# Two products of the receptances in one VectorE instruction, masks by comparison, and a new order of the work, in a linear-attention kernel followed by a token mixer

## The chip, the cores and the metric

The kernel runs on one core of a Trainium2 chip. The time is the device time of one execution in microseconds (us). The kernel before has a median of 104.82 us in three runs (104.32 to 105.43). The profile is of one execution, which took 104.46 us. Its span, from the first to the last recorded work, is 102.6 us, so that 1.86 us of that execution lie around the span.

Engine names in the profile: PE is TensorE (PEld its weight loads), DVE is VectorE, ACT is ScalarE, POOL is GpSimd, SP is SyncE, which here issues nearly all of the transfers (DMA). PSUM is the memory that TensorE writes to; SBUF is the main memory on the core.

## What is computed

```python
# r, k, v, w: (4, 8, 768, 48) f32;  u: (8, 48)
state = zeros((B, H, D, D))
for t in range(S):
    cur = einsum('bhd,bhe->bhde', u[None] * kt, vt)
    y[:, :, t] = einsum('bhd,bhde->bhe', rt, state + cur)
    state = wt[:, :, :, None] * state + einsum('bhd,bhe->bhde', kt, vt)
x = y.transpose(0, 2, 1, 3).reshape(B, S, H * D)
W_tok = einsum('bsd,btd->bst', x @ w_q, x @ w_k) / sqrt(64)
out = maximum(einsum('bst,btd->bsd', W_tok, x), 0) @ w_out
```

The sequential state is replaced by chunks of 128 tokens: inside a chunk the products of r and k are a masked matrix, between chunks a state is carried.

## The kernel before, in words

The four batches have 768 tokens each. A unit is 256 tokens (two chunks, called c = 0 and 1) of one batch, with all eight heads, so that there are twelve units, 0 to 11, three for each batch. `unit` (L493) adds the steps of one unit to a plan; after the third unit of a batch it also adds the mixer of that batch (T, TS, mx, rl, fp, os, st). The first and the last unit are cut in two halves ("split") for most steps. The last four units (`PAIRS`, L236) load k and r with another assignment of tokens to partitions, and need a second set of masks and scales (CM2, US2, gx2, gv2, gk2).

The steps of a unit that matter here, with the buffer that each one writes:

- Loads of w, k, r, v into wg, kg, rg, vg: all on SP's queue, L306, L312 and L320. Each has a ring of four buffers. In units 0 to 7, k and r come in two halves; in units 8 to 11, v comes in four quarters.
- ln (L525): lw <- log of w, on ScalarE. cw (L549): running sums of lw by a product with the mask CM (or CM2). ep and en (L569, L575): the exponentials of plus and minus those sums, on ScalarE. ew (L582): a small copy inside ep, on GpSimd, not in units 8 to 11.
- k16 and r16 (L539, L536): casts of k and r to bf16. kT and rT (L591): their transposes on TensorE, left in PSUM.
- ks (L610, run in the helper at L437 or L443): copy of kT from PSUM to SBUF. qT = rT * ks (L614, VectorE). RT = rT * ep (L624, VectorE). KT = ks * en (L633, GpSimd or VectorE).
- v16, vp, VB (L649, L657, L661): v cast, put in order by a product with the permutation PM, and copied from PSUM; in units 8 to 11 only one cast (L644). dps, dd (L667, L674): sums of qT with u. Vd = VB * dd (L681, GpSimd).
- A (L693): products of KT and RT. AM (L701, VectorE): A times the mask US (or US2). kb, kd (L708, L714): KT transposed back and copied with the scale gk into a padded buffer. sn, SB (L732, L748): the carried state. yi, ya: products into the output of the unit. X (L807, VectorE): that output with Vd added, then xt, XT, qk, QK for the mixer.

Every name above is a ring of a few buffers (`RINGS`, L260), mostly two: a step that fills a buffer waits until the readers of the buffer two units back are done.

The order on each engine is not that of the program text. `Plan.add` (L47) records a step with the engines that may run it and an estimated duration; `Plan.order` (L80) plays all the queues, takes on each engine the steps in order of a written number (`RANK`, L165), and gives out PSUM banks. Where a step may run on several engines, the next letter of `ALT` (L202) chooses (A ScalarE, D VectorE, P GpSimd). L453 to L457 tell the plan at which time each engine comes out of set-up. `WARM` products of zeros (L944, "z") fill gaps on TensorE, beside nine in set-up.

`setup` (L325) makes the constants. VectorE sets Z, CM, IDP and ID to start values, makes the positions, clears the pads of lw, k, r, and clears PM and the pads of the two kd buffers (L368 to L371: the long one is 16 pieces of 80 bf16). GpSimd makes iotas and cuts CM, IDP and ID by affine selects (L344, L349, L357). Four further functions are steps of the plan and run on GpSimd where `RANK` puts them: the positions of the second set (L381), its masks (L392), its scales (L405, VectorE) and the permutation PM (L373).

Of the kernel before, what the change touches and what calls it, by code (L numbers as in the profile page):

```python
# [10 lines left out]
F32 = mybir.dt.float32  # L11
# [22 lines left out]
class Plan:  # L34
# [131 lines left out]
    0, 0, 0, 0, 63, 33, 0, 0, 33, 1, 2, 3, 14, 2, 5, 22, 13, 0, 0, 0, 1, 0, 0, 2, 0, 0, 3, 0, 0,  # L166
    4, 0, 0, 8, 0, 0, 1, 1, 2, 1, 3, 4, 4, 5, 7, 6, 4, 6, 3, 5, 6, 4, 7, 6, 9, 17, 11, 28, 16, 15,
    18, 12, 8, 16, 10, 10, 8, 21, 14, 23, 12, 25, 15, 26, 37, 34, 33, 21, 57, 33, 82, 46, 5, 0, 0,
    6, 0, 0, 7, 0, 0, 9, 0, 0, 10, 0, 0, 12, 0, 0, 7, 8, 11, 11, 9, 10, 10, 15, 20, 9, 13, 11, 12,
    13, 32, 19, 38, 22, 22, 27, 16, 31, 18, 29, 18, 36, 20, 40, 22, 43, 46, 53, 49, 29, 66, 35,  # L170
    84, 43, 11, 0, 0, 13, 0, 0, 14, 0, 0, 15, 0, 0, 16, 0, 0, 20, 0, 0, 12, 14, 16, 24, 17, 17,
    15, 30, 35, 17, 19, 23, 19, 20, 45, 25, 50, 28, 26, 54, 30, 48, 27, 42, 24, 52, 28, 61, 63,
    64, 65, 37, 76, 42, 88, 45, 91, 48, 100, 51, 105, 54, 78, 0, 0, 106, 55, 138, 70, 67, 0, 0,
    118, 60, 160, 81, 81, 0, 0, 18, 0, 0, 17, 0, 0, 19, 0, 0, 24, 0, 0, 25, 0, 0, 26, 0, 0, 20,
    21, 24, 39, 24, 23, 23, 41, 56, 25, 32, 31, 26, 25, 58, 31, 62, 35, 32, 71, 40, 68, 38, 51,
    29, 59, 33, 69, 39, 73, 77, 81, 75, 44, 104, 53, 120, 63, 23, 0, 0, 21, 0, 0, 22, 0, 0, 27, 0,
    0, 29, 0, 0, 30, 0, 0, 26, 21, 27, 55, 30, 28, 32, 47, 60, 27, 34, 36, 31, 29, 67, 36, 79, 43,
    37, 78, 42, 83, 47, 74, 41, 80, 45, 87, 48, 90, 93, 96, 95, 52, 113, 62, 125, 64, 32, 0, 0,
    28, 0, 0, 31, 0, 0, 37, 0, 0, 38, 0, 0, 40, 0, 0, 34, 30, 41, 72, 38, 35, 39, 70, 86, 37, 50,
    49, 36, 38, 97, 50, 99, 54, 46, 101, 55, 92, 51, 94, 49, 102, 57, 111, 115, 112, 114, 63, 122,  # L180
    67, 139, 71, 145, 75, 154, 78, 172, 86, 82, 0, 0, 157, 80, 191, 98, 83, 0, 0, 171, 85, 201,
    101, 80, 0, 0, 35, 0, 0, 34, 0, 0, 36, 0, 0, 39, 0, 0, 44, 0, 0, 42, 0, 0, 40, 34, 39, 89, 47,
    42, 46, 85, 98, 44, 53, 58, 43, 45, 116, 58, 117, 59, 52, 109, 60, 124, 68, 107, 59, 121, 66,
    127, 69, 131, 136, 133, 135, 72, 144, 78, 153, 77, 47, 0, 0, 41, 0, 0, 43, 0, 0, 45, 0, 0, 46,
    0, 0, 50, 0, 0, 52, 40, 41, 108, 56, 47, 57, 103, 119, 56, 65, 64, 49, 48, 123, 62, 126, 65,
    53, 142, 77, 132, 71, 128, 66, 134, 73, 140, 76, 149, 151, 155, 152, 82, 168, 84, 186, 93, 51,
    0, 0, 48, 0, 0, 53, 0, 0, 54, 0, 0, 57, 0, 0, 68, 0, 0, 58, 0, 0, 61, 44, 51, 130, 67, 68,
    110, 137, 61, 74, 75, 54, 60, 146, 79, 62, 150, 81, 147, 80, 143, 73, 161, 86, 164, 166, 167,
    169, 90, 173, 88, 182, 91, 193, 99, 200, 100, 218, 110, 84, 0, 0, 212, 105, 226, 114, 85, 0,
    0, 215, 107, 229, 115, 86, 0, 0, 52, 0, 0, 49, 0, 0, 59, 0, 0, 55, 0, 0, 65, 0, 0, 69, 0, 0,  # L190
    70, 0, 0, 69, 50, 57, 141, 74, 72, 129, 156, 70, 84, 83, 56, 61, 175, 87, 65, 165, 89, 176,
    94, 159, 85, 163, 88, 174, 93, 177, 179, 181, 183, 97, 203, 102, 211, 104, 64, 0, 0, 56, 0, 0,
    61, 0, 0, 60, 0, 0, 76, 0, 0, 62, 0, 0, 71, 0, 0, 79, 55, 59, 162, 83, 82, 148, 170, 76, 91,
    92, 63, 64, 185, 92, 67, 188, 98, 180, 95, 178, 89, 184, 96, 189, 99, 192, 198, 194, 197, 105,
    204, 103, 214, 106, 75, 0, 0, 66, 0, 0, 79, 0, 0, 72, 0, 0, 74, 0, 0, 77, 0, 0, 73, 0, 0, 90,
    58, 66, 187, 95, 94, 96, 97, 158, 190, 87, 101, 100, 68, 102, 69, 70, 196, 104, 71, 72, 199,
    106, 206, 108, 195, 103, 202, 107, 205, 208, 207, 209, 210, 213, 109, 216, 111, 219, 222, 109,
    111, 110, 217, 112, 220, 221, 108, 112, 223, 225, 224, 113, 227, 113, 114, 231, 232, 117, 118,
    87, 0, 0, 89, 0, 0, 228, 115, 116, 233, 236, 118, 120, 88, 0, 0, 91, 0, 0, 230, 117, 116, 234,
    235, 119, 119, 121, 90, 0, 0, 2, 3, 5, 7, 8, 9, 13, 14, 18, 19, 44,  # L200
]
ALT = "ADDDDPAAAAADPPDPAAAAAPPDPAADAAAAAAAAAAPDDADAAAPPAPADDDAPAAPADADAAAAAAAAPPAPAADDAPPDPAAAAAPPDPDAAAAAAADAAPPDPADAAPPAPAAAAPPDPPDDDAADAADAAADDDAADADA"  # L202

WARM = 11
# [3 lines left out]
def kernel(  # L208
# [27 lines left out]
    PAIRS = (8,9,10,11)  # L236
# [56 lines left out]
    gx = const([C, 1], F32, "gx")  # L293
    gv = const([C, 1], F32, "gv")
    gk = const([C, 1], F32, "gk")

    US2 = const([C, C], F32, "US2")
    CM2 = const([C, 2 * C], BF16, "CM2")
    pos2 = const([C, 1], I32, "pos2")
    pos3 = const([C, 1], I32, "pos3")  # L300
    gx2 = const([C, 1], F32, "gx2")
    gv2 = const([C, 1], F32, "gv2")
    gk2 = const([C, 1], F32, "gk2")

    def load(b, i, tl, ap):
# [680 lines left out]
```

## Time and profile before

| what | before |
|---|---|
| median of three runs | 104.82 us |
| the profiled execution | 104.46 us |
| its span | 102.6 us |
| busy PE / DVE / ACT / POOL | 90.2 / 83.3 / 80.1 / 77.4 us |
| share of all DMA engines' time, the loads' queue | 83.0% |
| AM on DVE | 24 of 1220 ns |
| KT on POOL | 9 of 2127 ns, 3 halves of 1158 ns |
| KT on DVE | 1 of 1923 ns, 1 half of 426 ns |
| qT and RT on DVE, 1024 columns | 12 of 683 ns and 10 of 684 ns |

A line of a timeline has the start and the duration in us, the engine, the line of the kernel, the operation and what it writes and reads; a bracket at its end is the idle time before it and what ended that. A line of the chain has the start, the time and the place, and the chain is that of the work that ended last, followed back from the end. In the slices of the span, each digit is the busy share of a fortieth of the span, in tenths.

### The profile page before, as it was taken

The numbers are of one execution on the slowest core, as the hardware profiler recorded it, in microseconds if no ns is written. First come the engines' busy times: TensorE is split into PE (matmuls) and PEld (weight loads), VectorE is DVE, ScalarE is ACT, GpSimd is POOL, SyncE is SP. The second block draws the span as 40 slices with busy tenths as digits, with TensorE's granted clock in tenths as the row PEclk, the third lists the DMA queues.
The fourth block names the chain that finished last, engine by engine and source line by source line (L and its number), as shares of the span: only waits on it lengthen the run. The fifth ranks groups of instructions, "written<-read, shape, count | busy, mean of one in ns | idle before, by whom it ended". The sixth has DMA issues, their size and how long they took to land.

```text
span 102.6 us, 4039 instructions
## 1 busy us (share of the span) xinstructions
PE 90.2 (88%) x1647; PEld 67.8 (66%) x1648; DVE 83.3 (81%) x144; ACT 80.1 (78%) x124; POOL 77.4 (75%) x100
## 2 busy tenths in 40 slices
PE   5978698997969999999999999978999999999910
PEld 1245467765947878777789886756888677967600
DVE  6768799999999999799998989885989977738410
ACT  6375789999789969999898989756998949774730
POOL 5899999999999999999898997469886992000000
PEclk9999999999999999999999999999999999999996
DMA  2999999999999999799999999967970001954892
GB/s 39 287 294 347 334 333 276 323 336 327 322 289 299 336 318 301 217 290 320 250 238 215 209 225 233 311 121 136 292 224 11 0 0 50 364 209 160 310 369 90
DMA packets 46595, 24.65 MB, mean 240 GB/s; under 512 B 39152, under 2 KB 46448, under 8 KB 46576
## 3 DMA queue, kind: packets, MB, share of 16 engines
q1 hardware_dynamic: 46416, 24.19, 83.0%
q8 instruction: 13, 0.21, 0.7%
q10 hardware_dynamic: 160, 0.20, 0.5%
q14 instruction: 6, 0.05, 0.2%
HBM read 19.66 MB, written 4.72 MB: 238 GB/s over the span
## 4 chain that ended last, share of the span: by engine, by line
PE 49%; DVE 14%; DMA 8%; POOL 8%; ACT 6%; issue 6%; SPq 4%; POOLq 0%; ACTq 0%; DVEq 0%
PE PS L243 49%; DMA rg<-in_r_dram 5%; DVE AM L701 4%; DMA vg<-in_v_dram 3%; SPq L320 2%; DVE KT L633 2%; DVE ks L443 2%; POOL CM L397 2%; SPq L312 2%; DVE RT L624 1%; DVE SB L748 1%; DVE qT L614 1%; POOL PM L377 1%; POOL CM L344 1%; ACT QK L437 1%
## 5 line engine op out<-in xcount | busy, mean ns | idle before, releaser
L701 DVE TENSOR_TENSOR AM<-PS,US 128x1024 bf16<-128x1024 f32 x24 | 29.2, 1220 | 2.7 <-PE PS L243 2.4
L633 POOL TENSOR_TENSOR KT<-ks,en 128x1024 bf16<-128x1024 bf16 (+1 forms) x12 | 22.6, 1885 | 0.9 <-ACT en L575 0.9
L681 POOL TENSOR_TENSOR Vd<-VB,dd 128x768 bf16<-128x768 bf16 (+1 forms) x14 | 18.0, 1291 | 0.2
L569 ACT ACTIVATE ep<-PS 128x1024 bf16<-128x1024 f32 (+1 forms) x14 | 12.6, 907 | 1.6 <-PE PS L243 1.3
L575 ACT ACTIVATE en<-PS 128x1024 bf16<-128x1024 f32 (+1 forms) x14 | 12.7, 906 | 1.0 <-PE PS L243 0.9
L243 PE MATMUL PS<-wo,MX 128*128 128x384 bf16 x72 | 13.3, 326 | 0.0
L807 DVE SCALAR_TENSOR_TENSOR X<-PS,gx,Vd 128x768 bf16<-128x768 f32 (+1 forms) x13 | 12.4, 951 | 1.1 <-PE PS L243 1.1
L243 PEld LDWEIGHTS <-KT 48*128 48x128 bf16 (+1 forms) x272 | 11.0, 95 | 3.2 <-issue 1.2
L525 ACT ACTIVATE lw<-wg 128x768 bf16<-128x768 f32 x12 | 10.2, 846 | 2.7 <-DMA wg<-in_w_dram 2.6
L449 ACT ACTIVATE MX<-PS 128x768 bf16<-128x768 f32 (+1 forms) x12 | 8.7, 736 | 2.8 <-PE PS L243 2.7
L437 ACT COPY os<-PS 128x768 f32<-128x768 f32 (+1 forms) x12 | 8.3, 693 | 3.2 <-PE PS L243 2.6
L243 PE MATMUL PS<-RT,KT 48*128 48x128 bf16 x192 | 9.8, 216 | 0.1
L624 DVE TENSOR_TENSOR RT<-PS,ep 128x1024 bf16<-128x1024 bf16 (+1 forms) x14 | 8.5, 608 | 1.4 <-POOL ep L582 1.1
L243 PEld LDWEIGHTS <-MX 128*128 128x128 bf16 x72 | 6.8, 98 | 3.8 <-issue 0.3
L243 PE MATMUL PS<-Z 128*128 128x512 bf16 x19 | 7.2, 498 | 2.1 <-DVE Z L327 1.2
L243 PE MATMUL PS<-VB,AM 128*128 128x48 bf16 x192 | 8.3, 184 | 0.0
L243 PE MATMUL PS<-VB,kd 128*128 128x48 bf16 x160 | 7.2, 183 | 1.1 <-ACT VB L437 0.9
L614 DVE TENSOR_TENSOR qT<-PS,ks 128x1024 bf16<-128x1024 bf16 x12 | 8.2, 683 | 0.0
L243 PE MATMUL PS<-SB,RT 48*128 48x48 bf16 x160 | 7.0, 182 | 1.3
L243 PEld LDWEIGHTS <-kd 128*128 128x128 bf16 x160 | 6.6, 96 | 2.2 <-issue 1.9
L437 ACT CAST VB<-PS 128x768 bf16<-128x768 f32 x8 | 6.4, 798 | 2.1 <-PE PS L243 1.0
L748 DVE TENSOR_TENSOR SB<-PS,ep 128x192 bf16<-128x192 f32 x20 | 7.0, 351 | 1.2 <-PE PS L243 1.0
(106 smaller groups left out, 208.9 us busy)
## 6 DMA issues: line engine op xcount, KB each, us to landing
wg<-in_w_dram SPq DMA_DIRECT2D x12, 384.0 KB, 4.8
out_dram<-os SPq DMA_DIRECT2D x9, 384.0 KB, 3.2
kg<-in_k_dram SPq DMA_DIRECT2D x16, 192.0 KB, 4.6
rg<-in_r_dram SPq DMA_DIRECT2D x16, 192.0 KB, 4.2
vg<-in_v_dram SPq DMA_DIRECT2D x8, 384.0 KB, 5.2
kg<-in_k_dram SPq DMA_DIRECT2D x4, 384.0 KB, 5.0
rg<-in_r_dram SPq DMA_DIRECT2D x4, 384.0 KB, 5.0
vg<-in_v_dram SPq DMA_DIRECT2D x16, 96.0 KB, 4.8
```

What stands on the lines that cost most here:

```text
L243: return nc.tensor.matmul(o, l, rr, start=start, stop=stop, skip_group_check=True, is_transpose=trans)
L437: nc.scalar.copy(o, i)
L449: nc.scalar.activation(o, i, ACT.Relu)
L525: nc.scalar.activation(view(lw.tile, 0, [[64, H], [512, 2], [1, D]]), view(g["wg"].tile, 0, [[D2, H], [D, 2], [1, D]]), ACT.Ln, bias=0.0, ...
L569: nc.scalar.activation(view(ep.tile, o + 66, [[EW, n4], [-65, 2], [1, 64]]) if pairs else view(ep.tile, o + 16, [[EW, n4], [1, C]]), at(cw ...
L575: nc.scalar.activation(en.tile[:, ds(cs[0] * 512, w_)], at(cw)[:, ds(cs[0] * 512, w_)], ACT.Exp, bias=0.0, scale=-1.0)
L614: lambda e: nc.vector.tensor_tensor(qT.tile, at(rT, BF16), ks.tile, ALU.mult),
L624: nc.vector.tensor_tensor(view(RT.tile, cs[0] * 512, [[C, n4]] + cols), view(at(rT, BF16), cs[0] * 512, [[C, n4]] + cols), view(ep.tile, c ...
L633: x.tensor_tensor(KT.tile[:, cols], ks.tile[:, cols], en.tile[:, cols], ALU.mult)
L681: nc.gpsimd.tensor_tensor(Vd.tile[:, cols], VB.tile[:, cols], view(dd.tile, cs[0] * H, [[1, len(cs) * H], [0, D]]), ALU.mult)
L701: AMs[c] = add(("AM", n, c), {"D": 1221}, lambda e, c=c, A=A: nc.vector.tensor_tensor(view(AM[c].tile, 0, [[C, 8], [1, C]]), view(at(A), 0 ...
L807: nc.vector.scalar_tensor_tensor(view(X.tile, (2 * i + c0) * DM, [[DM, nc_], [1, DM]]), view(at(y), 0, [[512, nc_], [1, DM]]), gx_, view(V ...
```

## The change

What changes, in four parts.

1. In units 1 to 7 ("one"), qT and RT become one instruction. ks now lies behind ep in one buffer, ek, with the same row step EW = 144, and RT and qT lie in one buffer, RQ. rT is read twice by a step of 0. In the other units RT and qT stay two instructions. The new instruction waits for rT, ks and ep (with ew).
2. CM, CM2, US2 come from comparisons of an iota of the columns (TC, TC2) with the token number of the partition on VectorE, in set-up, in place of affine selects on GpSimd. All of the second set's making moves into set-up: gx2 and gv2 on ScalarE, gk2 on VectorE.
3. In set-up, PM's and the kd buffers' clearing moves from VectorE to GpSimd, and so does the making of the permutation, which was a step of the plan.
4. `RANK` and `ALT` are replaced as wholes, and `WARM` is 9 in place of 11.

```diff
-        ep=(2, 8 * EW, BF16), en=(2, 1024, BF16), ks=(2, 1024, BF16), qT=(2, 1024, BF16),
-        RT=(2, 1024, BF16), KT=(2, 1024, BF16), ...
+        ek=(2, 16 * EW, BF16), en=(2, 1024, BF16), RQ=(2, 2048, BF16), KT=(2, 1024, BF16), ...
...
-        nc.vector.memset(CM, 1.0)
+        nc.gpsimd.iota(view(TC2, 0, [[64, 2], [1, 64]]), pattern=[[1, 2], [2, 64]], base=0,
+                       channel_multiplier=0)
         for c in range(2):
-            for j in range(2):
-                m = view(CM, j * C, [[16, 8], [1, 16]], p0=c * 64, pn=64)
-                nc.gpsimd.affine_select(m, m, pattern=[[1, 8], [8, 16]], compare_op=ALU.is_ge,
-                                        fill=0.0, base=-j, channel_multiplier=-2)
+            nc.gpsimd.iota(tok[ds(c * 64, 64), :], pattern=[[0, 1]], base=0, channel_multiplier=2)
...
+        nc.vector.tensor_copy(tokf, tok)
+        nc.vector.tensor_scalar_add(tok1, tokf, 1.0)
+        nc.vector.tensor_scalar(CM[:, ds(0, C)], TC, tokf, None, ALU.is_ge)
+        nc.vector.tensor_scalar(CM[:, ds(C, C)], TC, tok1, None, ALU.is_ge)
+        nc.vector.tensor_copy(pos2[ds(0, 64), :], tokf[ds(0, 64), :])
+        nc.vector.tensor_copy(pos2[ds(64, 64), :], tok1[ds(64, 64), :])
+        nc.vector.tensor_scalar_add(pos3, pos2, 1.0)
...
+        nc.scalar.activation(gx2, pos2, ACT.Exp, bias=0.0, scale=MU)
+        nc.scalar.activation(gv2, pos3, ACT.Exp, bias=0.0, scale=-MU)
...
-        nc.vector.memset(PM, 0.0)
+        nc.gpsimd.memset(PM, 0.0)
+        permute()
         for x in tiles["kd"]:
-            nc.vector.memset(x[:, ds(0, 64)], 0.0)
-            nc.vector.memset(view(x, 64 + D, [[128, 16], [1, 128 - D]]), 0.0)
+            nc.gpsimd.memset(x[:, ds(0, 64)], 0.0)
+            nc.gpsimd.memset(view(x, 64 + D, [[128, 16], [1, 128 - D]]), 0.0)
+        nc.vector.tensor_scalar(US2, TC2, pos2, gv2, ALU.is_gt, ALU.mult)
+        nc.vector.tensor_scalar(CM2[:, ds(0, C)], TC2, tokf, None, ALU.is_ge)
+        nc.vector.tensor_scalar(CM2[:, ds(C, C)], TC2, tok1, None, ALU.is_ge)
+        nc.vector.tensor_scalar_mul(gk2, gv2, UNIT)
...
-        x = add(("pairs", 0), {"P": 700}, lambda e: by_pairs_positions())
-        x = add(("pairs", 1), {"A": 500}, lambda e: by_pairs_decays(), [x])
-        y = add(("pairs", 2), {"P": 2300}, lambda e: by_pairs_masks())
-        wts["c2"] = y
-        wts["m2"] = add(("pairs", 3), {"D": 320}, lambda e: by_pairs_scaled(), [x, y])
-        wts["p"] = add(("pm",), {"P": 900}, lambda e: permute())
...
+        RT, KT = ring("RQ"), ring("KT")
+        qT, Q0 = RT, 1024
+        one = not split and not pairs and True
...
+            def f_RQ(e):
+                nc.vector.tensor_tensor(
+                    view(RT.tile, 0, [[Q0, 2], [C, 8], [1, C]]),
+                    view(at(rT, BF16), 0, [[0, 2], [C, 8], [1, C]]),
+                    view(ep.tile, 0, [[KS, 2], [EW, 8], [1, C]]), ALU.mult)
```

The new `RANK` and `ALT` move steps between engines and in their queues. In the order in which the two built programs issue their work:

| step | before | after |
|---|---|---|
| ks copies | DVE 8, ACT 4 | DVE 5, ACT 7 |
| KT | POOL 9 and 3 halves; DVE 1 and 1 half | POOL 7 and 3 halves; DVE 3 and 1 half |
| casts of k and r | POOL 20, ACT 2, DVE 2 (unit 0) | POOL 24 |
| kd copies | DVE 3 and 2 halves; ACT 4 and 4 halves | DVE 5 and 2 halves; ACT 2 and 4 halves |
| VB copies | ACT 8 | ACT 7, DVE 1 |
| dd copies | DVE 5, ACT 7 | DVE 2, ACT 10 |
| MX | ACT 9 and 3 halves; DVE 3 halves | ACT 8 and 1 half; DVE 1 and 5 halves |

The three whole KT on DVE after are those of units 1, 3 and 5. On SP's queue the first eleven loads keep their order (w0, k0, r0, w1, k1, v0, r1); later ones are reordered: the halves of k and r of unit 2 come before v1, and the last loads are quarters of v for units 10 and 11, with outputs between them, where before the last load was r of unit 11.

## The prediction

> **What bounds the kernel now.** I read the page's slices first, then the chain in order of time, then the timelines of VectorE and GpSimd.
>
> ```profile
> PE 90.2 (88%) x1647; PEld 67.8 (66%) x1648; DVE 83.3 (81%) x144; ACT 80.1 (78%) x124; POOL 77.4 (75%) x100
> PE   5978698997969999999999999978999999999910
> DVE  6768799999999999799998989885989977738410
> POOL 5899999999999999999898997469886992000000
> DMA  2999999999999999799999999967970001954892
> ```
>
> There is no single bound. POOL is full from the second slice on, DVE from 12 to 40 us, PE from about 30 us to the end, and the transfers without a gap until two thirds of the span. So what counts is who hands the work on late.
>
> ```profile
> 1.97 0.35 POOL CM L344
> 5.10 0.64 POOL PM L377 x2
> 6.17 0.85 POOL CM L397 x2
> 8.62 0.46 POOL US L402
> 10.68 0.24 POOL ep L582
> 10.95 0.42 DVE RT L624
> 11.37 1.13 DVE AM L701
> ...
> 32.65 5.49 DMA rg<-in_r_dram
> ...
> 66.28 2.65 DMA vg<-in_v_dram
> ...
> 87.03 10.35 PE PS L243 x110
> ```
>
> The chain starts on GpSimd: masks, permutation and second masks until 9.12, then the small copy into ep, for which RT waited 1.09 us. From there it is DVE until 25 us. Later it passes twice through a load, and from 69.84 to 97 us it is PE alone.
>
> ```profile
> 6.26 0.61 DVE L539 CAST k<-kg 128x768 bf16<-128x768 f32 x1 [0.48 <-DMA kg<-in_k_dram]
> 23.49 1.92 DVE L633 TENSOR_TENSOR KT<-ks,en 128x1024 bf16<-128x1024 bf16 x1
> 28.81 0.68 DVE L624 TENSOR_TENSOR RT<-PS,ep 128x1024 bf16<-128x1024 bf16 x1
> 29.41 0.68 DVE L614 TENSOR_TENSOR qT<-PS,ks 128x1024 bf16<-128x1024 bf16 x1
> 81.13 0.41 DVE L624 TENSOR_TENSOR RT<-PS,ep 128x512 bf16<-128x512 bf16 x1
> 81.46 0.68 DVE L614 TENSOR_TENSOR qT<-PS,ks 128x1024 bf16<-128x1024 bf16 x1
> ```
>
> Instructions on DVE overlap: the next starts 0.60 us after a product of 1024 columns that is busy for 0.68. This step from start to start is what a full engine pays, and I use it below.
>
> ```profile
> 5.79 0.31 POOL L393 MEMSET CM<- 128x256 bf16 x1
> 8.01 0.20 POOL L399 MEMSET US<- 128x128 f32 x1
> 23.39 1.48 POOL L681 TENSOR_TENSOR Vd<-VB,dd 128x768 bf16<-128x768 bf16 x1
> 24.81 0.75 POOL L582 COPY ep<-ep 128x120 bf16<-128x120 bf16 x1
> ```
>
> The first two give GpSimd's memset: 256 elements 0.312 us, 128 elements 0.204, so 0.096 + 0.84 ns for each element. The other two belong to the long KT on DVE.
>
> **One product for two.** The start-to-start steps are 0.60 for 1024 columns and 0.33 for 512, so 0.27 for each 512 and 0.06 that is fixed. One instruction of 2048 columns steps 1.14 where two took 1.20: 0.06 in each of seven units, 0.42 us in all. The page "VectorE: DVE Perf Modes" of the Trainium skill (Side-by-side: where the cycles go for N=2048 bf16) gives each instruction about 150 cycles of start and 8 of fill, which would make it 0.165 us a unit, 1.15 in all (an estimate). The busy times say nearly that (683 + 684 against about 1220), but that fixed part overlaps the neighbour here, so I take 0.42. In exchange RT waits for ks, and qT for ep: before, qT of unit 2 started at 19.68 and RT at 21.79, 2.1 us apart. Between 0 and 2.1 us for a unit, near 0 where the new order has both early; I take nothing, since AMs and SBs stand ahead of it in DVE's queue and cover it.
>
> **Set-up on GpSimd.** Removed: CM's selects (1.4), four iotas (0.5), the second masks (5.79 to 9.12, 3.3). Added: one iota of 128 columns (0.25), two of one column (0.25), PM's clearing (0.31), and the kd pads, 1280 bf16 each: 0.096 + 1280 x 0.84 ns = 1.17, twice, with two of 64 (0.15): 2.6 us. On DVE these pads were 0.59 each, since there they were written as 640 uint32; the built program keeps 80 x 16 bf16 on GpSimd (packed the same way they would be 0.63 each, end of the range 1.1 lower). Walk from 0.89: iotas to 1.8, IDP and ID selects to 2.35, PM's clearing to 2.7, four selects (4.42 to 5.79 before, 1.37) to 4.1, pads to 6.7. So GpSimd is free at 6.7, not 9.12.
>
> **Set-up on DVE** loses 1.8 us (CM, PM, pads), gains some ten operations of 0.1 to 0.3: about 5.5 against 5.78, hidden, as k lands at 6.24. ScalarE gets two of 0.19 ahead of lw, which waits for w until 4.20: nothing. Later 0.7 us of US2 and gk2 leave DVE.
>
> **Unit 0.** Its casts move from DVE (0.61, 0.56, at landing) to GpSimd (0.82 each) behind the pads: k 6.7 to 7.5, kT at 7.55 (6.93 before), r 7.5 to 8.3, rT to 8.97 (8.48), ks 8.25 to 8.93 (7.71 to 8.39). The change gives back 0.55 us here. Both ew are done by 8.7, two us earlier. Then DVE: half KT at 9.0, RT twice, qT, AM at 10.6; before, AM started at 11.29. Second AM to 12.9 (14.16 before, with ks of unit 1, 0.60, ahead of it).
>
> **Unit 1.** ks to 13.5, KT on DVE to about 14.3, SB 0.27, the joint product 1.15, SB, kd 0.53, two AM 2.26: 18.7. r of unit 1 allows it: its load keeps its place and was landed by 12.63. Before, the same point (second AM of unit 1) was 19.76, with ks of unit 2 done; that copy is ScalarE's now. Lead: **1.05 us**.
>
> **The lock.** The half KT on DVE took 0.43, the whole one 1.92. GpSimd's Vd ran 23.39 to 24.87, and KT ended 25.41, 0.54 later; the ep copy behind it took 0.75 where its fellows take 0.28. The skill's page "SBUF — State Buffer" (Who interferes with whom, and the list under the two sides) says that a VectorE operation with two SBUF inputs and a GpSimd operation that reads SBUF exclude each other for a whole instruction. This speaks against the change, which runs three whole KT on DVE instead of one. By the rule the wait is up to GpSimd's longest, 2.13 (its own KT); by the row 1.38; with GpSimd's casts of 0.82 and copies of 0.28 also in play, I take 0.6 each. At 9.0 us DVE's half KT and GpSimd's half KT start on the same event: if GpSimd wins, DVE stands still for 1.1 us and the lead of 1.05 is gone.
>
> **Units 2 to 4, DVE** (from there to the second AM of unit 4). After: 3 joint products 3.42, 7 SB 1.9, 4 X 3.8, 6 AM 6.8, 2 KT 1.1 + 1.2 of lock, 2 kd 1.06, one XT 0.46: 19.7. Before: 3 RT and 3 qT 3.6, 6 SB 1.6, 4 X 3.8, 6 AM 6.8, KT 1.85, ks 0.6, kd 0.9, dd and QK 0.7: 19.8, and 0.9 of waits, 20.67 measured. The re-sorting is a draw. GpSimd loses 2 KT (4.2) and gains 4 casts (3.1); ScalarE gains three ks (2.7), loses two casts (1.5), two kd (1.6), one VB (0.7), some MX (1.5). Both get a little room, so I take a third of the waits: 0.3.
>
> **The rest.** From 40 us PE and the loads set the pace; PE's products are the same. Two fillers of zeros less cost nothing: they ran where PE waited, and the granted clock is full in all slices but the last. The late loads are reordered: v of units 10 and 11 last, r and w of unit 11 earlier. v's way to TensorE is the shortest, but its quarters queue on SP behind outputs that wait for ScalarE's os. Between minus 1.0 (PE's idle 65 to 70 recovered) and plus 1.5; I take 0.
>
> **Sum**: 1.05 + 0.3 = 1.35 us from a span of 102.6: 101.25, with 1.86 around it 103.1. That execution was 0.36 below the median of the runs; on the median it is 103.5. I say **103.3 us**.
>
> **Rivals.**
> - *The loads hide it*: the loads' queue takes 83% of the span, their share is about full until 66 us, PE waits at 66 to 70 for k and v. A lead then becomes idle time at 66 us: 104.4. Against it: between 10 and 37 us no engine stood waiting for a load.
> - *The lock decides* (slower): GpSimd wins at 9.0 (+1.1), and units 1, 3 and 5 pay 1.4 as the one row does, not 0.6 (+2.4 together): 103.3 + 3.5 = 106.8 at the worst, about 106 with one of the four places spared. It decides from 1.9 us of lock beyond what I took, when 103.3 becomes slower than before by the bound used here.
> - *The joint product does nothing*: only 0.42 us of DVE are lost, which the draw above contains; it would not change a sign.
>
> **How the numbers follow.** A measurement of this kernel tells about 1% from no change. The forecast has 0.50 (its own range 102.3 to 104.0), the loads 0.22, the lock 0.28. A little of the first lies above 103.77, so faster 0.48, same 0.25, slower 0.27. The range goes from 101.4 (packed pads or PE's idle time recovered, 1.1 each, mostly one of them) to 106.3.
>
> **What would show it.** After: GpSimd's first cast near 6.7 with pads of 1.17; first AM near 10.6; second AM of unit 1 near 18.7; seven joint products of about 1.22 busy; KT on DVE with a mean near 1.2 for whole ones; PE idle at 66 to 70 not grown. I am wrong if the pads are short, if the first half KT on DVE takes over 1 us, or if the lead at 19 us is gone at 70.

## The result, and the profile after

The changed kernel takes 106.1 us (median of 20 executions, 104.96 to 107.84), the kernel before beside it 104.55 us (20 executions, 103.58 to 107.02). The ratio is 1.0148, with a 95% interval of 1.0119 to 1.0177: 1.5% slower, where I had forecast 1.4% faster. The profiled execution took 107.22 us with a span of 105.4 and is one of the longer ones; the ratio counts, on both sides, only executions within 1.5% of the quickest of their kernel.

TensorE's clock fell in that execution (a mean of 0.984), but this is not what makes the changed kernel slower: four of its 20 executions have a mean clock of 1.0, and they took 105.87 to 106.16 us.

The page's busy times and slices, to lay beside those of before:

```profile
PE 93.4 (89%) x1646; PEld 69.0 (65%) x1646; DVE 85.1 (81%) x142; ACT 78.5 (74%) x120; POOL 75.8 (72%) x94
PE   5979998999879988899998999969999999999740
POOL 7999979996879986799579998699957956000000
PEclk9999999999985999999999999999999999999999
```

GpSimd, full without a break before, now has gaps in the second quarter; TensorE has 8s there; its clock has an 8 and a 5 (0.66 as a mean from 30 to 35 us). The chain in order of time (start, time, place) has lost the masks at its start, and loads and GpSimd stand in their place:

```profile
11.40 4.41 DMA rg<-in_r_dram
...
28.64 0.84 POOL v L646
...
36.60 3.78 DMA kg<-in_k_dram
...
62.50 4.41 DMA rg<-in_r_dram
```

Ahead of the first of these lines the chain is SP issuing loads back to back, mostly 0.59 to 0.60 us each and up to 1.26, from 0.71 to 11.36. SP's share of the chain is 16% (4% before), that of the transfers 12% (8%).

The set-up and unit 0 went as forecast, but for one thing. The timelines of VectorE and GpSimd:

```profile
3.82 0.37 DVE L378 TENSOR_SCALAR US<-TC,posf,gv 128x128 f32<-128x128 int32 x1
4.07 1.43 DVE L384 TENSOR_SCALAR US<-TC,pos,gv 128x128 f32<-128x128 int32 x1
4.25 1.17 POOL L383 MEMSET kd<- 128x1280 bf16 x1
6.79 0.82 POOL L520 CAST k<-kg 128x768 bf16<-128x768 f32 x1
```

The pads take 1.17 and 1.28 us, and GpSimd is free at 6.79. While they run, VectorE's second US takes 1.43 us; its twin, just ahead, took 0.37. Four such operations end VectorE's set-up at 6.8 us. It costs nothing here, as the next one waits for TensorE until 8.32.

The lead ends in unit 1, at its second AM (lines of GpSimd, TensorE and VectorE):

```profile
13.80 2.15 POOL L678 TENSOR_TENSOR Vd<-VB,dd 128x384 bf16<-128x384 bf16 x2 [0.57 <-ACT dd L425]
15.90 0.82 POOL L520 CAST k<-kg 128x768 bf16<-128x768 f32 x1
16.66 0.82 POOL L520 CAST r<-rg 128x768 bf16<-128x768 f32 x1
17.55 0.62 PE L243 MATMUL PS<-IDP,r 128*128 128x128 bf16 x8
18.10 0.40 PE L243 MATMUL PS<-RQ,KT 48*128 48x128 bf16 x8
18.61 1.23 DVE L698 TENSOR_TENSOR AM<-PS,US 128x1024 bf16<-128x1024 f32 x1 [0.73 <-PE PS L243]
```

The products A for this AM (PE's second line) stand in TensorE's queue behind kT and rT of unit 2 (the first is rT), which need GpSimd's casts of k and r of unit 2; and GpSimd is at Vd of unit 0 until 15.95.

The timeline from 25 to 30 us shows how the work is handed on late further back:

```profile
25.83 0.82 POOL L520 CAST r<-rg 128x768 bf16<-128x768 f32 x1 [0.84 <-DMA rg<-in_r_dram]
26.48 0.72 DVE L619 TENSOR_TENSOR KT<-ek,en 128x1024 bf16<-128x1024 bf16 x1
26.59 1.29 POOL L520 CAST k<-kg 128x768 bf16<-128x768 f32 x1
28.15 1.22 DVE L612 TENSOR_TENSOR RQ<-PS,ek 128x2048 bf16<-128x2048 bf16 x1 [0.95 <-POOL ek L565]
28.64 0.83 POOL L646 CAST v<-vg 128x768 bf16<-128x768 f32 x1 [0.52 <-PE PS L243]
29.52 0.50 PE L243 MATMUL PS<-v,PM 64*128 64x384 bf16 x4 [0.95 <-POOL v L646]
```

The cast of r waits for its load, the cast of k is held up by KT on VectorE (1.29 us instead of 0.82), so the small copy into ek comes late (27.84), the joint product waits 0.95 us for it, the cast of v is late, and TensorE stands still for 0.95 us. X(2) starts at 29.29, 2.8 us ahead of before; X(3) at 40.40, 2.8 behind. (The new order puts each X at another place among the other work, so these are not leads and lags of the whole.)

Two more views of this part. The first is the stretch from the second AM of unit 1 to that of unit 4, before and after (from and to, length, busy us and count of PE, PEld, DVE, ACT and POOL, clock, DMA share, GB/s):

```profile
19.76:40.44 20.68, 18.68 (x411) 15.08 (x408) 20.12 (x30) 18.29 (x25) 20.59 (x21) 1.00 1.05 319
19.84:42.54 22.70, 20.04 (x409) 15.93 (x410) 19.83 (x26) 19.08 (x28) 18.80 (x20) 0.92 0.96 285
```

VectorE is busy for less time than before, and yet the stretch is 2.0 us longer; GpSimd, busy in all of it before, now stands idle for 3.9 us. The second view is TensorE's busy time from 20 to 45 us, with the mean clock there and what the DMA engines moved.

| kernel, real loads | PE busy, 20 to 45 us | clock | GB/s |
|---|---|---|---|
| before | 22.92 | 1.00 | 305 |
| after | 22.39 | 0.93 | 285 |
| after, another execution | 19.95 | 1.00 | 288 |

0.07 less clock over 25 us is 1.7 us, so in both executions TensorE did 2.2 to 3 us less work in that stretch, once by a halved clock and standing still, once by standing still alone. This row is no exact account of the end, though: the new set-up in before's order (below) did 1.2 us less here and had a span of 102.9, only 0.3 longer.

### The profile page after: what moved, and what is told of

The parts are those of the page before. It is cut to its first block, busy times and chain, and to the rows that moved or that the text cites. A ratio compares the mean times of both kernels' runs of the same rounds, so it can differ in the third digit from the quotient of the medians.

```text
span 105.4 us, 4017 instructions
## 1 busy us (share of the span) xinstructions
PE 93.4 (89%) x1646; PEld 69.0 (65%) x1646; DVE 85.1 (81%) x142; ACT 78.5 (74%) x120; POOL 75.8 (72%) x94
## 4 chain that ended last, share of the span: by engine, by line
PE 48%; SPq 16%; DMA 12%; POOL 10%; issue 4%; DVE 4%; ACT 1%; POOLq 0%; ACTq 0%; DVEq 0%
PE PS L243 48%; SPq L315 10%; DMA rg<-in_r_dram 8%; POOL KT L619 4%; DMA kg<-in_k_dram 4%; SPq L309 3%; DVE AM L698 2%; SPq L323 2%; POOL v L646 2%; POOL r L520 1%; POOL k L520 1%; POOL k L517 1%; DVE X L804 1%; POOL r L517 1%; ACT VB L425 1%
## 5 line engine op out<-in xcount | busy, mean ns | idle before, releaser
L619 POOL TENSOR_TENSOR KT<-ek,en 128x1024 bf16<-128x1024 bf16 (+1 forms) x10 | 18.6, 1860 | 0.2 <-DVE ek L431 0.2
L552 ACT ACTIVATE ek<-PS 128x1024 bf16<-128x1024 f32 (+1 forms) x14 | 12.6, 912 | 3.0 <-PE PS L243 2.8
L243 PEld LDWEIGHTS <-RQ 48*128 48x128 bf16 (+1 forms) x256 | 8.1, 94 | 5.2 <-issue 4.1
L243 PE MATMUL PS<-RQ,KT 48*128 48x128 bf16 x192 | 9.6, 220 | 0.3 <-ACT VB L425 0.2
L612 DVE TENSOR_TENSOR RQ<-PS,ek 128x2048 bf16<-128x2048 bf16 x7 | 8.5, 1218 | 1.3 <-POOL ek L565 1.0
L520 POOL CAST r<-rg 128x768 bf16<-128x768 f32 x8 | 6.6, 825 | 2.8 <-PE PS L243 1.8
L745 DVE TENSOR_TENSOR SB<-PS,ek 128x192 bf16<-128x192 f32 x20 | 7.0, 352 | 1.9 <-PE PS L243 1.4
L243 PE MATMUL PS<-CM,lw 64*128 64x128 bf16 x192 | 8.0, 226 | 0.1
L520 POOL CAST k<-kg 128x768 bf16<-128x768 f32 x8 | 7.0, 880 | 1.5 <-DMA kg<-in_k_dram 1.4
L646 POOL CAST v<-vg 128x768 bf16<-128x768 f32 x8 | 6.6, 824 | 2.0 <-PE PS L243 1.2
```

What stands on the lines that cost most here:

```text
L243: return nc.tensor.matmul(o, l, rr, start=start, stop=stop, skip_group_check=True, is_transpose=trans)
L520: op(view(o.tile, 0, [[64, 2], [128, 8], [1, D]]), view(g[src].tile, 0, [[8 * D, 2], [D, 8], [1, D]]))
L552: nc.scalar.activation(view(ep.tile, o + 66, [[EW, n4], [-65, 2], [1, 64]]) if pairs else view(ep.tile, o + 16, [[EW, n4], [1, C]]), at(cw ...
L619: x.tensor_tensor(view(KT.tile, cs[0] * 512, [[C, n4], [1, C]]), view(ks.tile, KS + cs[0] * NP * EW, [[EW, n4], [1, C]]), view(en.tile, cs ...
L646: v16s = add(("v16", n), {"P": 826}, lambda e: nc.gpsimd.tensor_copy(view(v16.tile, 0, [[D, H], [DM, 2], [1, D]]), view(g["vg"].tile, 0, [ ...
```

## The experiments

My theory after the result was that the order of the instructions, not the new operations, costs the time, because it meets the loads at other moments. The rivals: the joint product and its waits; the set-up; the lock between VectorE and GpSimd; SyncE's order. The runs below are from several chips, so each is compared by its ratio to the kernel before on its own chip, or with those run beside it. The kernel before spreads widely on some chips (103.1 to 107.0 us on the first), and where the medians of all executions say something else than the ratio, they are given too.

### With the real loads

**The changed kernel once more, unaltered.**

> The changed kernel once more, unchanged, for a second profile: the first one shows a stretch from 30 to 35 us in which TensorE's granted clock is 0.66, and only part of its 105.4 us can be the change. All theories expect a span of 103.5 to 104.5 here, and the lead over the kernel before at the third unit's X (29.3 us against 32.1) turned into a lag by the fourth unit's X (40.4 against 37.6) again, only smaller by the 1.3 us that the low clock costs.

Measured: 107.37 us in its one execution, longer than I had expected, span 105.6, with a full clock. Its chain shows another cause than that of the first profile:

```profile
38.04 6.69 DMA vg<-in_v_dram
...
44.88 0.84 POOL v L646
```

TensorE's timeline has two waits there, the first for a cast of r, the second for this cast of v:

```profile
42.41 0.62 PE L243 MATMUL PS<-IDP,r 128*128 128x128 bf16 x8 [1.33 <-POOL r L520]
45.76 0.50 PE L243 MATMUL PS<-v,PM 64*128 64x384 bf16 x4 [1.67 <-POOL v L646]
```

A load of v took 6.69 us to land, and the cast behind it on GpSimd was late. TensorE was busy for only 2.76 of the 5 us from 40 to 45. From the second AM of unit 1 to that of unit 4 it took 21.94 us (20.68 before). So two executions lose about the same in two ways.

**The new set-up alone, in before's order.** First with the plan told of it (which moved 81 of 236 PSUM banks), then with the plan left as it was (none moved):

```diff
-        x = add(("pairs", 0), {"P": 700}, lambda e: by_pairs_positions())
+        x = add(("pairs", 0), {"P": 700}, None)
...
+        nc.gpsimd.memset(PM, 0.0)
+        permute()
```

> The kernel before with only the new set-up (masks by comparison, second set and permutation in set-up, kd pads on GpSimd); order of the work, engines and products as before. If the set-up is what costs, this is slower than before (105 to 106). If the set-up gives the lead of about 1 us that the trace shows at unit 0 and the loss comes from the new order, it is 103.5 to 104.3 where before is 104.6.

> The kernel before with nothing but the new set-up (masks by comparisons, kd pads, PM's clearing and the permutation on GpSimd ahead of the loop, position copies and decays early); the order of all later instructions, their engines and the choice of PSUM banks are those of before. Theory 'the new order of the instructions costs' (the set-up itself helps a little and its lead is eaten by late loads): within 1% of before, 104 to 105.5 us. Rival 'the set-up costs' (lost fillers, VectorE held up while GpSimd clears pads, other start of the loads): 1.5% slower or more, as the earlier version of this experiment, which had also moved PSUM banks, seemed to show with a wide interval.

Measured: the first 106.86 us, ratio 1.0187 (0.9993 to 1.0381); the second 106.42 us beside 105.84, too few executions for an interval. Neither shows a gain, and neither shows a loss beyond the spread (the medians of all are 1.7% and 0.5% above before's). In the first, AM(0,0) starts at 10.71 (11.29 before) and AM(1,0) is 1.05 us ahead, but k of unit 2 lands at 16.4 us, and at X(0) the lead is gone. In the second, TensorE is busy for 21.68 us from 20 to 45 (22.92 before).

**The joint product as two instructions.**

```diff
-        one = not split and not pairs and True
+        one = False
```

> The changed kernel with two instructions in place of the joint product in units 1 to 7 (RT, then qT right behind it on VectorE); all else as changed. If the joint product's wait for the later of its inputs costs, this is 104.5 to 105.3. If the loss is in the order of the work, it stays at 106 to 106.5, and a little above the changed kernel (0.4 us of VectorE).

Measured: 106.67 us, ratio 1.0275 (1.0164 to 1.0386); by the medians of all, 1.5% above before. Without the joint product it is as slow as with it, so the joint product is not the cause. (This edit also moved 90 of 234 PSUM banks.)

**The changed kernel with before's order on SyncE.**

> The changed kernel with the transfers on SP's queue in the order of the kernel before (loads and stores alone; the other engines keep the new order). If the new order of the loads is what costs (v of unit 3 and k of unit 6 land late in the trace, outputs ahead of the last quarters of v), this is 103 to 104.5. If the order on the computing engines costs, it stays at 106 or grows, since loads and uses then no longer fit.

Measured: 110.27 us, ratio 1.0597 (1.0477 to 1.0717). The loads' new order isn't what costs: with before's, the new order of the work is slower still. (This edit also moved 140 of 234 PSUM banks, so the 110.27 is not the loads' order alone.)

**The end of SyncE's queue.**

```diff
-  ... st(0) rg(11) wg(11) st(2) vg(11,0) vg(10,3) vg(10,1) vg(11,3) vg(11,1) st(3) vg(10,2) st(1) vg(11,2)
+  ... vg(10,3) vg(10,1) vg(10,2) rg(11) wg(11) vg(11,0) vg(11,3) vg(11,1) vg(11,2) st(0) st(2) st(3) st(1)
```

> The changed kernel with SyncE's queue altered from 66 us on: the last three quarters of v of unit 10, then r, w and v of unit 11 are issued first, and all outputs behind them. Of X(10)'s lag of 5.9 us against before, about 3 come only in this stretch. Theory 'outputs in front of the last loads cost the end': X(10) starts near 86 to 87 and the time is 1 to 1.5 us below the changed kernel's, near 105. Rival 'the lag is made before 45 us and only carried': X(10) earlier, but the time within 0.5 us of the changed kernel's.

Measured: 106.86 us, ratio 1.0094 (1.0054 to 1.0134). That is about 0.5% less than the changed kernel's ratio, but the intervals overlap. X(10) starts at 88.43 us, not at 86 to 87, and stands 9.0 us behind X(9), as in the changed kernel: the outputs ahead of the last loads aren't what makes it late. TensorE's work from 20 to 45 us is 21.07 us. This profile is of an execution of 106.13 us, near the changed kernel's median, with a clock of 1.0 there, and up to 60 us it issues the changed kernel's work in the changed kernel's order. It takes 22.95 us from the second AM of unit 1 to that of unit 4 (20.68 before), with VectorE busy for 19.54: the loss ahead of the end isn't peculiar to the two long executions above.

### With quick loads

To take the loads' lateness away, every load was made to read contiguous pieces: same bytes, same issues, same queue. The tokens then lie on other partitions, so the output is another one, and SyncE's issue of a load becomes quicker too (0.33 us instead of 0.60).

```diff
     def load(b, i, tl, ap):
         nc.sync.dma_start(
-            out=view(tl, 0, [[D2, H], [1, D2]]),
-            in_=ap[b, :, ds(i * U, U)].rearrange("h (p j) d -> p h (j d)", j=2))
+            out=view(tl, 0, [[1, HW]]),
+            in_=dataclasses.replace(ap, offset=(b * H * S + i * U * H) * D, ap=[[HW, 128], [1, HW]]))
```

> The kernel before with every load of w, k, r and v reading pieces of 3072 (or 1536) contiguous bytes for each partition instead of runs of one token; bytes, issues and their order are unchanged. It puts other tokens on the partitions, so what is computed is not the reference's. Theory 'the loads set the pace of both kernels': about 3 us faster than before, 100 to 103. Rival 'the instruction order sets the pace': within 1% of before.

> The changed kernel with the same loads of contiguous pieces, and the same thing left out as in the companion on the kernel before. Theory 'the order matters only through what the loads deliver late': the gap of 1.5% between the two kernels closes or turns round, as the forecast lead of 1.3 us comes through: 99 to 102 us. Rival 'the order of after is worse by itself': 1.5 to 2 us above its companion.

Measured: before 102.17 us, ratio 0.9683 (0.9595 to 0.9771); the changed kernel 107.24 us, ratio 1.0114 (1.0062 to 1.0167). Quick loads bring the one 3% and the other next to nothing: my theory as I had stated it fell, for the gap should have closed. The timeline of the changed kernel with quick loads tells why (GpSimd's rows among VectorE's and TensorE's):

```profile
26.47 3.41 DVE L617 TENSOR_TENSOR KT<-ek,en 128x1024 bf16<-128x1024 bf16 x1
26.51 0.28 POOL L563 COPY ek<-ek 128x120 bf16<-128x120 bf16 x1
26.74 1.59 POOL L644 CAST v<-vg 128x768 bf16<-128x768 f32 x2
28.29 0.28 POOL L563 COPY ek<-ek 128x120 bf16<-128x120 bf16 x1
28.52 0.82 POOL L518 CAST r<-rg 128x768 bf16<-128x768 f32 x1
29.94 1.04 PE L243 MATMUL PS<-ID,KT 128*128 128x128 bf16 x8 [2.43 <-DVE KT L617]
```

With v and r there in time, GpSimd runs five operations without a break, and KT on VectorE stands still through all of them: 3.41 us for work of 0.69, ending 0.54 us after the last. TensorE waits 2.43 us for it. Then its clock goes. A table by stretches (from and to, length, PE busy and count, clock, DMA share, GB/s):

```profile
25.00:30.00 5.00, 2.46 (x63) 0.92 1.08 355
30.00:35.00 5.00, 4.90 (x52) 0.50 1.03 373
35.00:40.00 5.00, 5.00 (x66) 0.55 0.95 329
```

From 30 to 40 us TensorE is busy nearly without a gap at half speed, which is some 4.8 us of lost work. None of the 20 executions of this kernel kept a full clock (where it fell is on record for this one alone): the mean is near 0.983, 0.968 or 0.952 in all but one, in even steps, and the time rises as it falls (105.8 to 107.0 us at 0.98, 107.9 to 108.2 at 0.952, with one of 110.6). The page "TensorE: Matmul & The Clock Gate" of the Trainium skill (Part 1: The HAM clock gate) says that the clock is either whole or half and is decided anew in windows of about 3.4 us by how busy TensorE has been. A step of 0.0155 in 104 us is 3.2 us at half clock: the steps agree with it. Its threshold for the fall, one idle window, does not quite: here 2.43 us of standing still were enough.

The unit-1 lines of this run answer a question from above, whether the lead ended there for a late load:

```profile
15.91 0.82 POOL L518 CAST k<-kg 128x768 bf16<-128x768 f32 x1
18.62 1.23 DVE L696 TENSOR_TENSOR AM<-PS,US 128x1024 bf16<-128x1024 f32 x1 [0.73 <-PE PS L243]
```

With the real loads the last of the four loads for these casts landed at 15.8 us, with quick loads at 14.2, and the second AM of unit 1 starts at the same time: it is GpSimd's queue, with Vd of unit 0 ahead of the casts, that ends the lead, not the load.

### Without the lock

RT, which reads rT from PSUM, kept its 0.68 us beside a busy GpSimd (684 ns as a mean of ten before). So KT on VectorE was made to read kT from PSUM, from which ks is a copy.

```diff
+                i = view(ks.tile, KS + cs[0] * NP * EW, [[EW, n4], [1, C]])
+                if e == "D":
+                    i = view(at(kT, BF16), cs[0] * 512, [[C, n4], [1, C]])
-                x.tensor_tensor(view(KT.tile, cs[0] * 512, [[C, n4], [1, C]]),
-                                view(ks.tile, KS + cs[0] * NP * EW, [[EW, n4], [1, C]]),
+                x.tensor_tensor(view(KT.tile, cs[0] * 512, [[C, n4], [1, C]]), i,
```

> The kernel before with the KT products that stand on VectorE (a half one of unit 0, a whole one at 23.5 us) reading their first operand from PSUM, where the transpose left it, instead of from its copy ks in SBUF; order, engines and PSUM banks are those of before. With one operand in PSUM the product should not be shut out by GpSimd: 0.69 us instead of 1.92. Theory 'the loads set the pace': within 0.5% of before. Rival 'the lock costs what it takes': 1.2 us (1.1%) faster.

> The changed kernel with its four KT products on VectorE reading from PSUM; order, engines and banks are those of the changed kernel. In its profile these products lost only 0.65 us to GpSimd, so by the theory 'late loads and the idle time they cause' the time is within 0.5% of the changed kernel's, 1 to 1.5% above before. Rival 'the lock decides', with a price that varies between executions: 1.5 us lower, level with before.

> The changed kernel with loads of contiguous pieces (other tokens on the partitions, so not the reference's values) and KT on VectorE read from PSUM. With quick loads alone the KT at 26.5 us took 3.41 us, TensorE stood still for 2.4 us behind it, and the granted clock fell to 0.50 to 0.55 from 30 to 40 us. Theory 'the lock made the idle time, and the idle time brought the clock down': KT 0.69, clock 1.0, and 102 to 104 us. Rival 'the order is slow by itself': above 105 us.

> The kernel before with loads of contiguous pieces (other tokens on the partitions, so not the reference's values) and KT on VectorE read from PSUM: the companion of the run above. Its KT at 23.5 us took 1.80 us with quick loads, and TensorE waited 0.4 us for it. If TensorE's idle time is what counts: 0.4 us below the 102.2 us with quick loads alone.

Measured: a whole KT on VectorE takes 0.68 to 0.69 us in all four, in the third of them beside the same casts that held it before:

```profile
25.10 0.83 POOL L518 CAST k<-kg 128x768 bf16<-128x768 f32 x1
25.71 0.68 DVE L620 TENSOR_TENSOR KT<-PS,en 128x1024 bf16<-128x1024 bf16 x1
26.10 1.61 POOL L646 CAST v<-vg 128x768 bf16<-128x768 f32 x2
```

With quick loads the theory holds: the changed kernel falls from 107.24 to 103.25 us (103.04 to 103.45) with a clock of 0.992 to 1.0. These two ran on different chips; by their ratios (1.0114, and 0.9863 with an interval of 0.9789 to 0.9937) the gain is 2.5%. Before goes from 102.17 to 101.66, which its ratios don't tell from nothing (0.9683, 0.9716). With the real loads nothing of it comes: before 106.2 us, ratio 1.0121 (1.0039 to 1.0204), the changed kernel 106.89, ratio 1.0207 (1.0120 to 1.0294). I had not expected the first of these: an edit that only shortens one instruction of before, by 1.2 us, brings no gain. How much slower it is stays unsure, 1.2% by the ratio and 0.5% by the medians of all (106.2 and 105.64). From 20 to 45 us TensorE's work is 21.46 us there, 22.92 in before; its longest wait lies later, at 70 us, 1.5 us for a cast of k on GpSimd (0.8 before). In the changed kernel the edit brings a wait of its own: TensorE stands still for 1.18 us at 41 us, until KT has read the bank that is to be filled again. The last run below is free of that.

### The parts of the change, one by one, with quick loads and without the lock

In this setting most executions of a kernel agree within some 0.3 us, so that parts can be weighed. The four below ran side by side; the PSUM banks of the changed kernel were chosen anew for the longer use of kT.

> The kernel before with loads of contiguous pieces (other tokens on the partitions, not the reference's values) and KT on VectorE from PSUM once more, as the foot for the three runs beside it: 101.5 to 101.8 us.

> The same two alterations (and the same values left out) on the kernel before with the new set-up alone, in before's order. By the forecast the set-up frees GpSimd 2.4 us earlier and brings the first AM 0.6 us forward. Theory 'without late loads and without the lock the lead comes through': 0.5 us below its foot, about 101.1. Rival 'the lead is used up in the order that follows, whatever the loads do': level with the foot within 0.2 us.

> The changed kernel with the same two alterations (and the same values left out), with the PSUM banks chosen anew so that none is asked for while KT still reads it; in the run before, TensorE stood still for 1.2 us behind the KT at 36.3 us, whose bank was to be filled again. Theory 'that wait belongs to the experiment': 0.7 us below 103.25, so 102.5, and a rest of about 1 us above the foot that is the order's own. Rival 'the order of after makes TensorE wait there anyway': 103.2 again.

> As the run before, with the joint product as two instructions one behind the other. In this quiet setting the joint product's own worth should show: 0.42 us by the start-to-start step of the trace of before, 1.15 us by the fixed part that the page on VectorE's performance modes states for each instruction; nothing if VectorE is not what the end waits for.

| quick loads, no lock | median, us | PE busy, 20 to 45 us |
|---|---|---|
| before | 101.67 | 23.59 |
| before with the new set-up | 101.19 | 23.50 |
| the changed kernel | 102.38 | 23.13 |
| the changed kernel, joint product as two | 103.66 | 22.67 |

Not all agree: of six executions each, one of before (103.18), two with the new set-up (102.04 and 102.19) and three of the last kernel stand apart from the rest, one of these at 139.68 us with a mean clock of 0.573, which nothing here explains.

The set-up brings 0.48 us. The banks cost the earlier run some 0.9 (103.25 against 102.38; they ran on two chips, where before took 101.66 and 101.67). The joint product: three executions with two instructions at a clock of 0.999 or 1.0 took 103.05 to 103.20, so one instruction saves about 0.7 us (the two profiled spans say 0.5); two more at 0.983 took 104.1 to 104.2. That kernel also has 127 of 234 PSUM banks in other places, which the 0.7 contains. What is left I put down to the order, with all that it brings (engines, queues, banks): 102.38 - 101.67 + 0.48 + 0.7 = 1.9 us, if the parts add up.

X(9) starts at 75.16 here, against 75.87 in before, and X(10) at 84.48 against 80.99, though again in another order of the other work. From 75 to 95 us TensorE stands still for 1.05 us, in before for 0.27. The last of it, in the timeline of the changed kernel:

```profile
92.14 2.53 DVE L437 TENSOR_SCALAR MX<-PS 128x384 bf16<-128x384 f32 x5 [1.80 <-PE PS L243]
92.73 0.49 ACT L435 ACTIVATE MX<-PS 128x384 bf16<-128x384 f32 x1 [1.59 <-DVE MX L437]
93.28 3.08 PE L243 MATMUL PS<-wo,MX 128*128 128x384 bf16 x18 [0.59 <-DVE MX L437]
```

The new order gives one half of MX(9) to VectorE and one to ScalarE; ScalarE begins only when VectorE's half is done, and TensorE's last products wait. The profile puts ScalarE's 1.59 us down to VectorE's half; whether the program or the chip sets that order was not tested.

### The end mended

```diff
-  ScalarE: ... TS(11) rl(9,1) os(8) os(9,0) ...      VectorE: ... rl(9,0) rl(10,0) rl(10,1) rl(11,0) rl(11,1) ...
+  ScalarE: ... TS(11) rl(9,0) rl(9,1) os(8) rl(11,1) os(9,0) ...      VectorE: ... rl(10,0) rl(10,1) rl(11,0) ...
-  TensorE: ... mx(9) mx(11) mx(10) ...
+  TensorE: ... mx(9) mx(10) mx(11) ...
```

with SyncE's end as in the earlier run.

> The changed kernel with quick loads and KT from PSUM (102.4 us; other tokens on the partitions, not the reference's values) and its end mended: both halves of MX(9) on ScalarE and the last half of MX(11) too, the products mx in the order 9, 10, 11, as before has them, and the last outputs on SyncE behind all loads. Up to X(9) the changed kernel was 0.7 us ahead there, from X(10) on behind. Theory 'the end of the new order eats the lead': 101.3, level with the set-up alone. Rival 'the end is set by TensorE's amount of work': 102.3.

> The changed kernel with its real loads, KT on VectorE from PSUM with banks chosen for it, and the same mended end. If each part brought here what it brings with quick loads, it would be 1.5 us below the changed kernel and level with before. Theory 'late loads make idle time wherever something moves': 0.5 to 1.5% above before all the same.

Measured: 103.09 us with quick loads, against 102.38 without the mending; 106.85 us with the real loads, ratio 1.0218 (1.0155 to 1.0281). With quick loads it is 20.9 us from X(9) to the end of TensorE's work, instead of 21.2, so the mending brings 0.3 there; with the real loads it brings nothing (20.9 us in the changed kernel too). In the kernel with quick loads the clock fell again at 30 to 35 us (0.66), in a stretch that the edit does not touch and that looks the same before it (TensorE busy for 4.33 of 5 us from 25 to 30; 4.35 in the unmended one, whose clock stayed at 1.0). Why the one falls and the other not is open. X(10) did not move (9.32 us behind X(9) in both).

No version was found that beats before with the real loads. The nearest, the new set-up in before's order, isn't told apart from it; every version with the new order of the work is slower than before, with the joint product or without, with either order of the loads, with the lock or without, with the end mended or not.

## Why the prediction was wrong, point by point

| step | forecast | measured |
|---|---|---|
| GpSimd free, pads | 6.7 us, 1.17 each | 6.79 us, 1.17 and 1.28 |
| VectorE's set-up ends | 5.5 us | 6.8 us, hidden |
| first AM; the second ends | 10.6; 12.9 us | 10.73; 13.08 us |
| second AM of unit 1 ends | 18.7 us, a lead of 1.05 | 19.84 us, a lag of 0.08 |
| joint product, busy | 1.22 us | 1.218 us |
| joint product, worth | 0.42 us by the trace, 1.15 by the page | about 0.7 us, with quick loads |
| whole KT on VectorE | mean 1.2 us | mean 0.91 us (0.69, 0.72, 1.31) |
| units 2 to 4, VectorE busy | 19.7 us with 1.2 of lock | 19.83 us (20.09) |
| units 2 to 4, VectorE's waits | 0.6 us (0.9 less a third) | 2.87 us (1.85) |
| units 2 to 4, in all | 0.3 us gained | 2.0 us lost (1.3) |
| the rest | 0 | 0.7 us lost (1.7) |

The last four rows are of the stretch between the second AMs of units 1 and 4, and from there to the end of the span; in brackets stands the second execution of the changed kernel.

**The first steps came out, and the lead did not last.** GpSimd's set-up, the casts, the pads and the first AM came within 0.2 us of the forecast; VectorE's set-up took 1.3 us longer, hidden. With quick loads and without the lock, where nothing else stands in the way, the set-up alone brings 0.48 us, and the joint product about 0.7, with 127 banks moved: more than the 0.42 taken from the trace and less than the 1.15 of the page.

**The step that failed first is unit 1.** I added up VectorE's operations, and that sum held to some 0.2 us until the last AM: the wait of 0.73 us ahead of it had no term. I wrote that r of unit 1 was there in time, and did not ask for k and r of unit 2, behind whose transposes TensorE's products for that AM stand. Those wait for two casts on GpSimd, and these for its Vd of unit 0, which ends at 15.95 us. The lead of 1.05 us ended there, with the real loads and with quick ones.

**The step that failed most is the term for the waits in units 2 to 4.** I compared sums of busy time on VectorE, called them a draw, and let the waits shrink by a third, to 0.6 us. The sum was right: 19.83 us of busy time against 19.7. The waits were not: 2.87 and 1.85 us in the two executions (0.56 before, by the same view), behind casts and copies that GpSimd hands over late and behind TensorE, which waits for the same. A sum of busy time doesn't contain that.

**The rival of the loads** was set at 0.22, because in before no engine waited for a load between 10 and 37 us. It put the idle time at 66 us and no loss above before. In the changed order loads came late much earlier (in the first profile GpSimd waits 0.84 us for r ahead of 25.83 and 1.40 us for k ahead of 40.59, in the second 2.52 us for v ahead of 44.88), but late loads are not all of it, since quick ones didn't close the gap. I now read a load queue at a share of 1.0 with nobody waiting as no reserve: perhaps this order takes each load just when it lands. That is argued, not shown. Two edits that save local time inside before's order, the new set-up (1.05 us of lead) and KT from PSUM (1.2 us), gave no gain that could be measured.

**The rival of the lock** was right as a mechanism and wrong in its places. In the changed kernel's profile the three whole KT lost 0.65 us together, less than I took; GpSimd's gaps there leave the lock less to bite on. With quick loads it bit once, for 2.7 us where I had allowed 1.4. With the real loads, taking the lock away brings nothing (1.0207, and 1.0218 with the bank's wait gone and the end mended), so it isn't the cause of the 1.5%. One sum there is off too: after slower than before by 1% would be 105.87 us, 2.6 above 103.3, and not 1.9.

**The clock** had no price in the forecast. I had only used that it was full in all slices of before but the last. A gap on TensorE can be paid twice, by the wait and then by a few microseconds at half speed. But the clock isn't the 1.5% either: the executions of the changed kernel with a mean clock of 1.0 took 105.87 to 106.16 us, 1.3 to 1.5% above before's median, and the new set-up in before's order fell to 0.71 from 30 to 35 us in its first profile as well.

What is shown: the joint product, the lock and the order of the loads are not what costs with the real loads, and no loss from the set-up was found, so that the new order of the work is left as the cause, by exclusion. With quick loads, the lock and the clock behind it make most of the loss: 2.5% by the ratios, and 4.9 us by the medians (107.24 to 102.38, of two chips), in which choosing the banks anew has up to 0.9; some 1.9 us are left for the order. What stays open: through what the order costs 1.5% with the real loads, and how that divides between late loads, GpSimd's queue and standing still, since each edit there shifts the loads as well. Less was moved from 20 to 45 us in the changed order (285 to 288 GB/s, 305 before), and it isn't settled whether that is a cause or follows from the later casts.

## What to carry to other kernels

Price a re-sorting by what each queue hands over and when the next loads land, not by sums of busy time: in the forecast the busy time was right and the waits were not. Don't count a lead at the start as time at the end; follow it through the other engines' queues, here GpSimd's. To weigh the parts of such a change, make the loads quick first (contiguous pieces, same bytes); there, 0.5 us could be told apart, with the real loads 1 us hardly. A VectorE product of two SBUF operands beside a busy GpSimd waited once for a whole train of its operations: read one operand from PSUM where it lies there, and give its bank the longer use.

## What the hardware showed that I had not expected

- The lock need not be handed over after one instruction. With quick loads KT waited through five GpSimd operations, 26.51 to 29.34 us, and took 3.41 us; I had taken from the page "SBUF — State Buffer" of the Trainium skill (Who interferes with whom) that one instruction's length is the most. In before it was handed over after one: KT came ahead of the small copy into ep (0.75 us instead of 0.28). What decides is open.
- While GpSimd cleared the pads, which reads nothing, VectorE's four operations beside it (a twin of the first took 0.37 us) took between 1.13 and 1.43 us, and each pair ended within 0.2 us of a clearing's end. That page says that VectorE's two-port forms, which `tensor_scalar` can take, contend with GpSimd; I had applied the rule to KT alone. Which form these took, no run shows.
- TensorE's clock fell to half behind 2.43 us of standing still, in a stretch with 2.46 of 5 us busy, and stayed there for some 10 us though TensorE was then busy nearly without a gap. How busy TensorE is doesn't decide it alone: before kept a full clock behind 3.61 busy of 5 us (25 to 30), the changed kernel fell behind 3.94.
